# Where the second pieces of a Fourier step stand among the matmuls of a feed-forward layer (spectral mixer with a gated GELU branch, one core)

## The chip, the cores and the metric

The kernel runs on one core of a Trainium2 chip. The metric is the device time of one launch in microseconds (us); lower is better. Beside the plain runs there is one profiled execution, from which all traces are read.

## The reference

Inputs are `x` of 2 batches × 4096 tokens × 640 channels, the mixer weights `w1, b1, w2, b2` in four blocks of 160 channels, the feed-forward weights `w_gate, w_up` (640 × 1728) and `w_down` (1728 × 640), and a gate vector.

```python
g = sigmoid((x * gate_w).sum(-1, keepdims=True))
Xf = rfft2(x, axes=(1, 2))            # one row: a real transform over the 4096 tokens
# two complex block-diagonal layers on Xf: relu after the first, soft threshold 0.01 after the second
a = irfft2(Yf, s=(1, 4096), axes=(1, 2))
b = (gelu(x @ w_gate) * (x @ w_up)) @ w_down
return g * a + (1 - g) * b
```

## The kernel before

All matrix products run on TensorE with float32 operands that are split into a high and a low part, so each product of two matrices is three matmuls (high·high, high·low, low·high). A block product of one level of a Strassen-like scheme saves some of them. The high part is made by ScalarE (`high`, L274), the low part by VectorE (`low`, L277).

The kernel runs through these stages, and one program order per engine is written out by hand:

- **Up-projection.** `keys` (L1190) lists 48 passes, called keys here: three groups of weights (`groups`, L1189: 4, 4 and 6 column pairs), each with 16 token blocks. Keys 0 to 15 are the first group, 16 to 31 the second, 32 to 47 the third. A key runs `quad` (L487) once for each column pair (4, 4 and 5 times), and in the third group `mixed` (L559) once after its second quad. Key 0 runs `plain` instead. A quad issues 54 matmuls of 128x256, in seven products; a product is one call of `run` (L467) with 9 or 6 matmuls that add up in one PSUM bank. In the order of issue they are X (9), half5 of the quad before (9), C (9), A (6), X again (9), half3 of the quad before (6) and half4 of the quad before (6). All these matmuls have line L469 in the profile.
- **Stage A** is the first step of the Fourier transform. It has 64 token pairs (`a_seq`, L1192). Each needs an input load (`a_load`), two splits (`a_split`, one on each half of the partitions: a high of 64x640 on ScalarE and a low on VectorE), a gate sum (`a_gate`, VectorE), and two pieces (`a_step` with h=0 and h=1). A piece is two matmuls of 128x320 (L614), each followed by a ScalarE copy (L615) and a VectorE addition (L616); the second piece ends with a store. These are not a stage in time: they are put into the gaps between products of the up-projection.
- **Places.** A quad has seven hooks, one after each product or half; hook k of quad q of a key is slot 7q + k. `slots` holds what is called there. `A_POINTS` (L1235) gives the five slots of a token pair by weight group: split, split, gate, first piece, second piece. `steps_a` (L1246) says which key takes which token pair. The same slots carry the preparation of the next key's inputs (`x_prep`), of the next group's weights (`w_prep`) and of the down-projection's weights (`wd_pre`, in keys 33 to 46, at slots 12, 17, 22 and 27 of the odd keys and 1, 6, 11, ... 31 of the even ones).
- **PSUM.** There are eight banks. X and C of a quad and of the one before are open at the same time; A and each matmul of a piece take one more until VectorE has read them.
- **Queues.** SyncE issues most transfers; GpSimd issues the tables of stage A (`f1_load`, one for every 20 token pairs) and the stores of the prepared inputs in the first group.
- After key 47 follow the block-diagonal layers with the first inverse step, and then the second inverse step with the down-projection (`down`, L1139, which also uses `run`). The change moves nothing there.

Before, a key of the second group (17 to 30) has two token pairs and a key of the third group (33 to 44) has three; the first group has none. Both pieces stand at a hook, that is between two products.

Of the kernel before, what the change touches and what calls it, by code (L numbers as in the profile page):

```python
# [213 lines left out]
def spectral_mix_kernel(ctx: ExitStack, tc: tile.TileContext, a):  # L214
# [3 lines left out]
    def dr(t, off, ap):  # L218
        return bass.AP(tensor=t.tensor, offset=t.offset + off, ap=ap)
# [7 lines left out]
    def bank():  # L227
        return psum.tile([P, 512], F32, name="bank", tag="bank")
# [13 lines left out]
    def small(shape, dt=F32, name="small"):  # L242
        return pool.tile(shape, dt, name=name, tag="small", bufs=18)
# [7 lines left out]
    def st(dst, src):  # L251
        late.append((dst, src))
# [207 lines left out]
    def prod(ws, x):  # L460
# [3 lines left out]
            ops += [(wh, xh), (wh, xl), (wl, xh)]  # L464
        return ops

    def run(dst, ops, first=True):  # L467
        for i, (l, r) in enumerate(ops):
            nc.tensor.matmul(dst, l, r, start=first and i == 0, stop=i == len(ops) - 1, skip_group_check=True)  # L469

    def h_store(tp, t, h):
        st(dr(hD, 4 * tp * P * 14 * P + t * P, [[14 * P, P], [P * 14 * P, 4], [1, P]]),
           h.rearrange("p (t n) -> p t n", t=4))
# [13 lines left out]
    def quad(key, t, hook):  # L487
# [8 lines left out]

        X = half()
        run(X, prod(w["g1"], x_of(o, "b11", ("k4", 0))))
        p1 = T("p1")
        copy(p1, X)  # L500
        hook(0)
        old[0]()
        hook(1)
        C = half()
        run(C, prod(w["s3"], x_of(o, "t3", ("k4", 1))))
        hook(2)
        A = half()
        run(A, prod(w["g2"], x_of(o, "b21")))
        nc.vector.tensor_add(p1, A, p1)  # L509
        hook(3)  # L510
# [65 lines left out]
    def f1_load(q):  # L576
        m = min(5, 17 - 5 * q)
        F1[q] = big([P, 5, 2, P], F32R, name="f1")
        nc.gpsimd.dma_start(F1[q][:, :m], a["f1"][:, 5 * q:5 * q + m])
# [5 lines left out]
    def a_load(b, n2):  # L585
        t = small([P, D], name="xr")
        ld(t, a["x"][b, n2])
        XR[b, n2] = t

    def a_split(b, n2, h):  # L590

        t = XR[b, n2]
        xs = small([P, D], F32R, name="xs")
        hi, lo = (slice(0, 64), slice(64, P))[::1 - 2 * h]
        high(xs[hi], t[hi])
        low(xs[lo], t[hi], xs[hi])
        XS[b, n2, h] = xs

    def a_gate(b, n2):
        t = XR.pop((b, n2))  # L600
        nc.vector.scalar_tensor_tensor(t, t, 1.0, GW[0], op0=OP.mult, op1=OP.mult, accum_out=G[:, b, n2:n2 + 1])

    def a_step(b, n2, h):
        xs = XS.pop((b, n2, h))
        m = n2 if n2 < 16 else 32 - n2
        f = F1[m // 5][:, m % 5]
        if h == 0:
            XS[b, n2] = small([P, D], name="as")
        stg = XS[b, n2]
        hi, lo = (slice(0, 64), slice(64, P))[::1 - 2 * h]  # L610
        for q in range(2):
            cs = slice(320 * q, 320 * q + 320)
            pa = bank()
            nc.tensor.matmul(pa[:, :320], f[:, h], xs[:, cs], start=True, stop=True)  # L614
            nc.scalar.activation(stg[hi, cs], pa[lo, :320], AF.Copy)  # L615
            nc.vector.tensor_add(stg[hi, cs], pa[hi, :320], stg[hi, cs])  # L616
        if h:
            st(dr(scr1[b], n2 * D, [[32 * D, 4], [P * D, 32], [1, D]]), XS.pop((b, n2)))
# [613 lines left out]
    slots = {}  # L1232


    A_POINTS = {1: ((1, 3, 4, 5, 8), (12, 14, 16, 21, 23)), 2: ((0, 2, 3, 4, 9), (14, 15, 18, 18, 19), (24, 25, 27, 28, 29))}  # L1235

    points = lambda i: 7 * (5 if keys[i][0] == 2 else 4)

    def spread(i, s, fs):

        for k, f in enumerate(fs):
# [1 line left out]
            while j < last and q >= points(j):  # L1243
                j, q = j + 1, q - points(j)
            slots.setdefault((j, q), []).append(f)
    steps_a = [(i, j) for i in (*range(17, 31), *range(33, 46)) for j in range(2 if i < 33 else 3)][:64]  # L1246

    def back(i, s, f):
        if s < 0:
            i, s = i - 1, s + points(i - 1)  # L1250
        spread(i, s, [f])
    for k, (b, n2) in enumerate(a_seq):
        i, j = steps_a[k]
        sp = A_POINTS[keys[i][0]][j]
        if k in (0, 18, 38, 58):
            back(i, sp[0] - 12, lambda q=(k + 2) // 20: f1_load(q))
        back(i, sp[0] - 9, lambda b=b, n2=n2: a_load(b, n2))
        for s, f in zip(sp, (lambda b=b, n2=n2: a_split(b, n2, 0), lambda b=b, n2=n2: a_split(b, n2, 1),
                             lambda b=b, n2=n2: a_gate(b, n2), lambda b=b, n2=n2: a_step(b, n2, 0),
                             lambda b=b, n2=n2: a_step(b, n2, 1))):  # L1260
            back(i, s, f)
    for k in range(1, 4):
        spread(0, (0, 7, 14)[k - 1], w0[k][:2])
# [70 lines left out]
    for ch in range(1, 2 * NCH):  # L1334
        b, c = chunks[ch]
# [24 lines left out]
    for i in range(S + 2):  # L1360
# [18 lines left out]
        if 0 <= i - 1 < S:  # L1379
            b, c, n = steps[i - 1]  # L1380
# [66 lines left out]
```

## Time and profile before

| | us |
|---|---|
| median of 3 runs | 2575.9 (2572.92 to 2578.98) |
| profiled execution | 2586.86 |
| its span | 2585.1 |
| first and last piece of stage A (L614) start at | 446.0 and 1300.3 |
| TensorE busy in the span | 2568.1 |
| VectorE busy | 2062.9 |
| ScalarE busy | 1500.7 |
| GpSimd busy | 374.7 |

How to read it: the span is the time from the first to the last instruction of the profiled execution, and its own device time is 1.8 us longer. Matmuls are pipelined. A matmul is busy for some 280 ns, but the next one starts after less than half of that, so what counts for time is the distance from start to start, which a view gives as a stretch divided by the matmuls in it. A weight load (PEld) goes ahead of each matmul and overlaps the matmul before it. The granted clock is the share of its full clock that TensorE was given. A window of the trace also counts the instructions that were under way at its edges, so its counts are one or two above those that start in it.

### The profile page before, as it was taken

The numbers are of one execution on the slowest core, as the hardware profiler recorded it, in microseconds if no ns is written. First come the engines' busy times: TensorE is split into PE (matmuls) and PEld (weight loads), VectorE is DVE, ScalarE is ACT, GpSimd is POOL, SyncE is SP. The second block draws the span as 40 slices with busy tenths as digits, with TensorE's granted clock in tenths as the row PEclk, the third lists the DMA queues.
The fourth block names the chain that finished last, engine by engine and source line by source line (L and its number), as shares of the span: only waits on it lengthen the run. The fifth ranks groups of instructions, "written<-read, shape, count | busy, mean of one in ns | idle before, by whom it ended". The sixth has DMA issues, their size and how long they took to land.

```text
span 2585.1 us, 54281 instructions
## 1 busy us (share of the span) xinstructions
PE 2568.1 (99%) x20276; PEld 2560.5 (99%) x20276; DVE 2062.9 (80%) x4208; ACT 1500.7 (58%) x3490; POOL 374.7 (14%) x374
## 2 busy tenths in 40 slices
PE   9999999999999999999999999999999999999999
PEld 9999999999999999999999999999999999999999
DVE  7666567777778777777757788887899999999998
ACT  5444455666666566666645777777645444444443
POOL 0000000000000000000002111111233333333332
PEclk9999999999999999999999999999999999999999
DMA  6454547676667677776767354548744444344442
GB/s 216 161 192 164 188 166 236 205 239 212 218 213 250 197 231 232 242 222 218 237 202 222 121 165 142 162 141 249 284 148 154 153 145 141 130 153 153 146 135 99
DMA packets 341323, 483.48 MB, mean 187 GB/s; under 512 B 24572, under 2 KB 213500, under 8 KB 341060
## 3 DMA queue, kind: packets, MB, share of 16 engines
q1 hardware_dynamic: 326372, 438.47, 53.0%
q0 software_dynamic: 14688, 41.56, 4.4%
q8 instruction: 159, 2.61, 0.4%
q14 instruction: 104, 0.85, 0.1%
HBM read 300.29 MB, written 179.64 MB: 186 GB/s over the span
## 4 chain that ended last, share of the span: by engine, by line
PE 97%; DMA 1%; DVE 1%; ACT 0%; issue 0%; SPq 0%; DVEq 0%; ACTq 0%
PE bank L469 78%; PE bank L294 14%; PE bank L778 3%; PE bank L614 1%; PE bank L856 1%; PE bank L855 1%; DMA raw<-in_w1m_dram 0%; PE bank L858 0%; DMA zl<-zl 0%; DMA wx<-wdf 0%; DMA sc<-scr 0%; DMA rs<-in_w1s_dram 0%; DMA wraw<-in_wgu_dram 0%; DVE xo L278 0%; DVE s2s L278 0%
## 5 line engine op out<-in xcount | busy, mean ns | idle before, releaser
L469 PE MATMUL bank<-xo,w 128*128 128x256 f32 x11736 | 1390.9, 280 | 9.2 <-ACT xo L275 5.1
L469 PEld LDWEIGHTS bank<-xo,w 128*128 128x128 f32 x11736 | 1380.0, 189 | 12.3 <-ACT xo L275 5.1
L469 PE MATMUL bank<-wx,ho 128*128 128x320 f32 x4608 | 680.5, 309 | 0.0
L469 PEld LDWEIGHTS bank<-wx,ho 128*128 128x128 f32 x4608 | 676.7, 188 | 0.0
L493 ACT ACTIVATE u<-bank 128x256 f32<-128x256 f32 x408 | 156.0, 382 | 264.8 <-PE bank L469 259.1
L278 DVE TENSOR_TENSOR ho<-hraw,ho 128x640 fp32r<-128x640 f32 (+3 forms) x384 | 283.9, 780 | 5.1 <-ACT ho L275 3.1
L275 ACT ACTIVATE ho<-hraw 128x640 fp32r<-128x640 f32 x320 | 166.7, 574 | 63.3 <-PE bank L469 42.4
L493 ACT ACTIVATE p<-bank 128x256 f32<-128x256 f32 x204 | 78.3, 384 | 174.0 <-PE bank L469 80.7
L535 DVE TENSOR_TENSOR u<-bank,u 128x256 f32<-128x256 f32 x204 | 86.1, 422 | 98.7 <-PE bank L469 97.6
L526 DVE TENSOR_TENSOR u<-bank,u 128x256 f32<-128x256 f32 x204 | 86.1, 422 | 94.0 <-ACT u L493 91.2
L278 DVE TENSOR_TENSOR xo<-xraw,xo 128x512 fp32r<-128x512 f32 x209 | 143.0, 685 | 11.1 <-ACT xo L275 10.4
L1134 ACT ACTIVATE uu<-bank,gs 128x320 f32<-128x320 f32 x120 | 54.8, 524 | 161.5 <-PE bank L294 158.4
L278 DVE TENSOR_TENSOR xs<-xr,xs 64x640 fp32r<-64x640 f32 x128 | 105.0, 820 | 46.3 <-ACT xs L275 43.2
L616 DVE TENSOR_TENSOR as<-bank,as 64x320 f32<-64x320 f32 x256 | 113.9, 484 | 30.1 <-ACT as L615 28.8
L294 PE MATMUL bank<-wm,h 128*128 128x320 f32 (+1 forms) x792 | 137.8, 309 | 0.0
L275 ACT ACTIVATE xo<-xraw 128x512 fp32r<-128x512 f32 x209 | 130.8, 626 | 6.4 <-DMA xraw<-in_xT_dram 5.0
L567 POOL MEMSET h<- 64x512 f32 x16 | 8.3, 522 | 772.3 <-DMA xraw<-in_xT_dram 339.8
L294 PEld LDWEIGHTS bank<-wm,h 128*128 128x128 f32 (+1 forms) x792 | 118.6, 185 | 1.2
L509 DVE TENSOR_TENSOR p<-bank,p 128x256 f32<-128x256 f32 x204 | 86.1, 422 | 41.5 <-PE bank L469 38.7
L275 ACT ACTIVATE ho<-hs 128x640 fp32r<-128x640 f32 (+1 forms) x128 | 72.5, 579 | 79.7 <-PE bank L469 62.7
L278 DVE TENSOR_TENSOR s2s<-s,s2s 128x320 fp32r<-128x320 f32 x128 | 113.6, 944 | 0.4 <-ACT s2s L275 0.3
L615 ACT ACTIVATE as<-bank 64x320 f32<-64x320 f32 x256 | 96.7, 427 | 12.2 <-PE bank L614 9.6
(155 smaller groups left out, 3474.3 us busy)
## 6 DMA issues: line engine op xcount, KB each, us to landing
xo<-xD SPq DMA_DIRECT2D x124, 512.0 KB
xraw<-in_xT_dram SPq DMA_DIRECT2D x225, 256.0 KB
hD<-h SPq DMA_DIRECT2D x224, 256.0 KB
hraw<-hD SPq DMA_DIRECT2D x128, 320.0 KB
xD<-xo POOLq DMA_DIRECT2D x64, 512.0 KB, 3.2
sc<-scr SPq DMA_DIRECT2D x65, 320.0 KB
xr<-in_x_dram SPq DMA_DIRECT2D x64, 320.0 KB
scr<-as SPq DMA_DIRECT2D x64, 320.0 KB
```

Source lines behind the costliest of these rows:

```text
L275: nc.scalar.activation(dst, src, AF.Copy, scale=scale)
L278: eng.tensor_sub(dst, src, hi.bitcast(F32))
L294: nc.tensor.matmul(dst, l, r, start=i == 0, stop=i == len(ops) - 1)
L469: nc.tensor.matmul(dst, l, r, start=first and i == 0, stop=i == len(ops) - 1, skip_group_check=True)
L493: copy = lambda d, s_: nc.scalar.activation(d, s_, AF.Copy)
L509: nc.vector.tensor_add(p1, A, p1)
L526: nc.vector.tensor_add(u4, C, u4)
L535: nc.vector.tensor_add(u2, C, u2)
L615: nc.scalar.activation(stg[hi, cs], pa[lo, :320], AF.Copy)
L616: nc.vector.tensor_add(stg[hi, cs], pa[hi, :320], stg[hi, cs])
L778: nc.tensor.matmul(pz[:, kp * P:(kp + 1) * P], SC[b, c, kp][:, o:o + P], ft, start=True, stop=True)
L1134: nc.scalar.activation(uu[n2][:, cs], pe[:, :320], AF.Copy, scale=gs[:, b, 0, n2:n2 + 1])
```

## The change

Three edits. The second pieces are no longer called at their slot: they are put on the list `inner`, and the next call of `run` issues them right behind its first matmul, that is between the first two matmuls of a product. Ten token pairs go into keys 4 to 13 of the first group, one for each key, with the points of the first group of slots. Keys 33 to 45 of the third group then have two token pairs each instead of three in keys 33 to 44; the middle set of points (14, 15, 18, 18, 19) is dropped. The number of token pairs stays 64 and no matmul is added or removed.

```diff
+    inner = []
+
     def run(dst, ops, first=True):
         for i, (l, r) in enumerate(ops):
             nc.tensor.matmul(dst, l, r, start=first and i == 0, stop=i == len(ops) - 1, skip_group_check=True)
+            while inner and i == 0:
+                inner.pop()()
...
-    A_POINTS = {1: ((1, 3, 4, 5, 8), (12, 14, 16, 21, 23)), 2: ((0, 2, 3, 4, 9), (14, 15, 18, 18, 19), (24, 25, 27, 28, 29))}
+    A_POINTS = {0: ((1, 3, 4, 5, 8),), 1: ((1, 3, 4, 5, 8), (12, 14, 16, 21, 23)), 2: ((0, 2, 3, 4, 9), (24, 25, 27, 28, 29))}
...
-    steps_a = [(i, j) for i in (*range(17, 31), *range(33, 46)) for j in range(2 if i < 33 else 3)][:64]
+    steps_a = [(i, j) for i in (*range(4, 14), *range(17, 31), *range(33, 46)) for j in range(1 if i < 14 else 2)]
...
                              lambda b=b, n2=n2: a_gate(b, n2), lambda b=b, n2=n2: a_step(b, n2, 0),
-                             lambda b=b, n2=n2: a_step(b, n2, 1))):
+                             lambda b=b, n2=n2: inner.append(lambda: a_step(b, n2, 1)))):
             back(i, s, f)
```

## The prediction

> **What bounds the kernel.** I read the page first, then the groups of matmuls by stretch, then the order of time around the pieces of stage A, and last single weight loads.
>
> ```profile
> PE 2568.1 (99%) x20276; PEld 2560.5 (99%) x20276; DVE 2062.9 (80%) x4208; ACT 1500.7 (58%) x3490; POOL 374.7 (14%) x374
> PEclk9999999999999999999999999999999999999999
> PE 97%; DMA 1%; DVE 1%; ACT 0%; issue 0%; SPq 0%; DVEq 0%; ACTq 0%
> ```
>
> TensorE makes 97% of the chain of waits and hardly ever stops, at the full granted clock. The change adds and removes no matmul. So it can move the time only through the distance from one matmul to the next, or through new stops. The distance is not the same everywhere (first rows: windows, with the elapsed us, TensorE busy and its count in front; then the groups of 128x256 matmuls in the same three windows):
>
> ```profile
> 53.50:445.90 392.40, 392.40 (x3333) 392.35 (x3332) 251.13 (x570) 191.53 (x474) 29.76 (x56) 1.00 0.55 188
> 805.14:829.62 24.48, 24.48 (x218) 24.48 (x217) 20.09 (x55) 15.67 (x43) 0.00 (x0) 1.00 0.85 283
> 961.20:1382.60 421.40, 421.40 (x3548) 421.10 (x3547) 300.68 (x672) 253.35 (x602) 10.02 (x21) 1.00 0.71 228
> ...
> L469 PE MATMUL bank<-xo,w 128*128 128x256 f32 x3333 | 392.9, 281 | 0.0
> L469 PE MATMUL bank<-xo,w 128*128 128x256 f32 x218 | 24.9, 276 | 0.0
> L469 PE MATMUL bank<-xo,w 128*128 128x256 f32 x3429 | 414.1, 281 | 0.0
> ```
>
> The first window is 392.4/3332 = 117.8 ns a matmul. The second is key 31 with its 4 × 54 = 216 matmuls: 24.48/216 = 113.3 ns. The same shape has two paces, 4.5 ns apart, both at clock 1.00 (the number before the last two), and the busier DMA (0.85 against 0.55) goes with the fast one. The mean of one matmul, 281 or 276 ns, tells them apart. Slow are keys 1 to 16 and most of keys 35 to 46; the second group is fast throughout, from the first piece of stage A on.
>
> **What switches the pace.** This is matmuls in order of time at that first piece (start, length to the last end, count):
>
> ```profile
> 441.76 4.40 PE L469 MATMUL bank<-xo,w 128*128 128x256 f32 x36
> 446.00 0.45 PE L614 MATMUL bank<-xs,f 128*128 128x320 f32 x2
> 446.29 2.89 PE L469 MATMUL bank<-xo,w 128*128 128x256 f32 x24
> 449.02 0.45 PE L614 MATMUL bank<-xs,f 128*128 128x320 f32 x2
> ```
>
> Start to start it is (446.00 − 441.76)/36 = 117.8 ns before and (449.02 − 446.29)/24 = 113.8 ns after: two matmuls of a piece switched it. In the third group most pieces do not:
>
> ```profile
> 1001.60 0.45 PE L614 MATMUL bank<-xs,f 128*128 128x320 f32 x2
> 1001.89 1.23 PE L469 MATMUL bank<-xo,w 128*128 128x256 f32 x9
> 1002.95 0.45 PE L614 MATMUL bank<-xs,f 128*128 128x320 f32 x2
> 1003.24 9.35 PE L469 MATMUL bank<-xo,w 128*128 128x256 f32 x78
> 1012.43 0.45 PE L614 MATMUL bank<-xs,f 128*128 128x320 f32 x2
> ```
>
> After 1003.24 it is 9.19/78 = 117.8 ns still. What differs is the place in a beat of three. In the slow pace every third weight load takes 192 ns, the others 187 or 188. These are the first weight loads of the pieces at 446.00 and at 1001.60, each from a window that holds no other:
>
> ```profile
> L614 PEld LDWEIGHTS bank<-xs,f 128*128 128x128 f32 x1 | 0.2, 192 | 0.0
> ...
> L614 PEld LDWEIGHTS bank<-xs,f 128*128 128x128 f32 x1 | 0.2, 188 | 0.0
> ```
>
> I counted all pieces that started in the slow pace, 57 of them. Six have the 192 ns load first, and all six switch to fast. In 50 the 192 ns load stands just ahead of the piece; none switches, and the beat keeps its place in the products. One stands just ahead of the 192 ns load:
>
> ```profile
> 928.18 0.46 PE L614 MATMUL bank<-xs,f 128*128 128x320 f32 x2
> 928.48 1.22 PE L469 MATMUL bank<-xo,w 128*128 128x256 f32 x9
> 929.53 0.45 PE L614 MATMUL bank<-xs,f 128*128 128x320 f32 x2
> 929.82 2.44 PE L469 MATMUL bank<-xo,w 128*128 128x256 f32 x20
> ```
>
> After it the pace stays slow (929.53 − 928.48 is 1.05 us for 9, 117 ns), but the beat has moved forward by one matmul, and the next piece switches. All 71 pieces that started in the fast pace left it fast. All products have 6 or 9 matmuls, multiples of three, so between products the beat always meets a piece in the same place. The kernel before puts every piece there: a beat with the wrong place stays slow for good.
>
> **Edit 1, the second piece behind the first matmul of a product.** It adds no instruction. ScalarE's copy and VectorE's addition keep their place in their queues, since the product's own result comes later in any case. A piece there meets the beat one matmul further on. Call the place of the 192 ns load in a product 0, 1 or 2. By the three rules a first piece switches place 0, moves 1 to 0 and leaves 2; a second piece switches 1, leaves 0, and moves 2 to 1. So from any place, pieces in turn reach the fast pace in at most five. That the rules hold inside a product is taken from the stream of matmuls being the same there; no trace of before shows it.
>
> **Edit 2, ten token pairs in keys 4 to 13.** The first stands at about 115 us. Three weight loads in a row there, the first of them the first of a product:
>
> ```profile
> L469 PEld LDWEIGHTS bank<-xo,w 128*128 128x128 f32 x1 | 0.2, 187 | 0.0
> L469 PEld LDWEIGHTS bank<-xo,w 128*128 128x128 f32 x1 | 0.2, 192 | 0.0
> L469 PEld LDWEIGHTS bank<-xo,w 128*128 128x128 f32 x1 | 0.2, 187 | 0.0
> ```
>
> This is place 1. The first piece of key 4 moves it to 0, the second leaves it, the first of key 5 switches. Before, it was the same slot of key 17 that switched, 12 keys later: 12 × 216 × 4.5 ns = **−11.7 us** if the fast pace holds. A stop can end it. In the slow pace there is already one in key 14, where the next weights are prepared:
>
> ```profile
> 383.78 9.39 PE L469 MATMUL bank<-xo,w 128*128 128x256 f32 x77
> ```
>
> That is (9.39 − 0.28)/76 = 119.9 ns, 0.16 us of stops. No piece follows until key 17. If it turns the pace, some 62 us or 525 matmuls are slow again, +2.4 us; I take half, **+1.2**.
>
> What the ten pairs cost VectorE there (durations by group, then the same 8.5 us from the start of a key in the first and in the second group; VectorE is the third busy time):
>
> ```profile
> L616 DVE TENSOR_TENSOR as<-bank,as 64x320 f32<-64x320 f32 x256 | 113.9, 484 | 30.1 <-ACT as L615 28.8
> L278 DVE TENSOR_TENSOR xs<-xr,xs 64x640 fp32r<-64x640 f32 x128 | 105.0, 820 | 46.3 <-ACT xs L275 43.2
> L601 DVE SCALAR_TENSOR_TENSOR xr<-xr,gw 128x640 f32<-128x640 f32 x64 | 52.3, 818 | 0.5
> ...
> 185.80:194.30 8.50, 8.50 (x75) 8.50 (x74) 4.83 (x11) 3.65 (x9) 0.53 (x1) 1.00 0.58 213
> 646.80:655.30 8.50, 8.50 (x76) 8.50 (x76) 6.88 (x16) 5.47 (x12) 0.00 (x0) 1.00 0.69 247
> ```
>
> A token pair is 4 × 0.484 + 2 × 0.820 + 0.818 = 4.4 us, of which 3.4 fall into this stretch: 4.83 + 3.4 = 8.2 of 8.5 us. It is full, fuller than the 6.88 of the second group, so VectorE may run up to 1 us late. What waits for it first is half4, whose C bank VectorE must have read after half5; 30 matmuls lie between, 30 × 0.113 = 3.4 us. So I price this at nothing, with that cover; without it each key stops for what exceeds it. The pieces' own matmuls and transfers only move: 20 pieces leave the third group. The input loads (10 of 320 KB), stores and the first table on the GpSimd queue fall where DMA is busy 0.55 instead of 0.71.
>
> **Edit 3, two pairs a key in the third group.** The slow matmuls there are about the 3,370 of its 3,429 in the window above that are not in four short fast stretches, so 15 us at 4.5 ns is what can be had. How a fast stretch ends:
>
> ```profile
> 1034.81 4.20 PE L469 MATMUL bank<-xo,w 128*128 128x256 f32 x33
> 1038.84 0.45 PE L614 MATMUL bank<-xs,f 128*128 128x320 f32 x2
> 1039.13 1.19 PE L469 MATMUL bank<-xo,w 128*128 128x256 f32 x9
> 1040.16 0.45 PE L614 MATMUL bank<-xs,f 128*128 128x320 f32 x2
> ...
> L469 PE MATMUL bank<-xo,w 128*128 128x256 f32 x4 | 0.6, 276 | 0.0
> L469 PE MATMUL bank<-xo,w 128*128 128x256 f32 x68 | 8.2, 282 | 0.0
> ...
> 1040.91 0.87 DVE L616 TENSOR_TENSOR as<-bank,as 64x320 f32<-64x320 f32 x2
> ```
>
> The fast pace of 1041.1 is gone by 1041.7. In between, product A needed the bank that the addition at 1040.91 frees, about 0.06 us late. These are slots 28 and 29 of an odd key, which stay. The jam ahead of it does not: the dropped middle pair stood at 1029 us, and the 33 matmuls from 1034.81 took 4.03 us, 0.14 more than 33 × 117.8 ns. Over the odd keys I take **−1** for such stops. But in a whole fast key product A comes some 20 matmuls × 4.5 ns = 0.09 us earlier still, so I expect odd keys to fall back at slot 30. If the beat lands in place 2, as here, the next four pieces do not switch, and the first of the next odd key does: slow for 27 + 300 + 42 = 369 of 600 matmuls, which leaves 4 us of gain with the tail after key 45; in place 0 the next piece switches, 12 us. No stop at all gives 15. Between these I take **−6**, nearer to the row.
>
> **The sum.** −11.7 + 1.2 − 1 − 6 = −17.5 us. On the profiled execution, 2586.9 (2585.1 and 1.8 around the span), that is 2569; the median of the plain runs lies 11 us below that execution, so I forecast 2575.9 − 17 = **2559 us**.
>
> **Rivals.** *Fast everywhere*: the odd keys don't fall back and key 14 neither; −11.7 − 15 − 1 = −28, 2548. For it: with the middle pair gone VectorE is less loaded; against: the 0.06 us above is tied to a weight form at slot 27 that stays. *Stops keep breaking the first group*: the pieces there make and break the fast pace by turns, half of 11.7 is lost, and the third group gains little: −5, 2571. *The pace does not follow the beat*: one shape has one spacing in plain runs, or a piece inside a product does not act as between two; then nothing is gained, 2576. For it speaks only that the profiled execution is one of several; against it, six of six switches at the 192 ns load.
>
> The Trainium skill, TensorE: Matmul & The Clock Gate, section Back-to-back issue gap, gives a single spacing by the shape for an isolated matmul, N/2.4 + 2.5 ns, 109 ns for 256 columns; by that rule order is worth nothing and the time stays. The trace shows 113.3 and 117.8 ns for one shape, so it does not agree.
>
> *Slower*: VectorE in keys 4 to 13 is late by more than the 3.4 us of cover, since its 8.2 of 8.5 us come on top of what the quad before left over. Then half4 stops in the first or second quad of each of the ten keys, the fast pace is never kept in that group (0 instead of −11.7), and the third group gives −6. It decides from 0.6 us a key on; at 1.4 us it is +14 − 6 = +8, 2584. Against it: VectorE is idle in 43% of that stretch now.
>
> **Chances.** Forecast 0.40, fast everywhere 0.22, stops 0.15, no effect 0.11, slower 0.12. The range of 2545 to 2576 leaves out the slower case, half of no effect and a little below. A change within 0.2% (5.2 us) cannot be told from none here. Faster by more: 0.40 + 0.22 + 0.10 of the stops = 0.72; same 0.15 (the rest of the stops and most of no effect); slower 0.13.
>
> **What would show it.** Keys 6 to 13 at a mean of 276 ns a matmul from about 141 us on, and key 12 at about 25.1 us instead of 25.4; 276 ns in the second group as before; 281 ns in the third group only behind slot 29 of odd keys. It is wrong if keys 6 to 13 stay at 281 ns, if pieces inside products leave the fast pace, or if VectorE ends waits of L469 there.

## The result, and the profile after

| | before | after |
|---|---|---|
| median of 20 plain runs, us | 2575.4 (2562.2 to 2586.2) | 2563.0 (2558.8 to 2571.4) |
| ratio | | 0.9961 [0.9948, 0.9975] |
| profiled execution, us | 2586.9 | 2565.8 |
| its span, us | 2585.1 | 2564.0 |

The change makes the kernel faster: by 12.4 us in the medians, by 21 us between the two profiled executions. By the interval of the ratio, which is not the quotient of the two medians, the gain is 6 to 13 us. That the medians and the profiled executions differ is part of the explanation. The plain times of before are also spread twice as wide as those of after.

The page of after begins with these lines (first the busy times, then the granted clock by slices, then the chain by engine):

```profile
PE 2546.6 (99%) x20276; PEld 2539.7 (99%) x20276; DVE 2059.0 (80%) x4208; ACT 1502.7 (59%) x3490; POOL 376.4 (15%) x374
PEclk9999999999999999999999999999999999999999
PE 96%; DVE 2%; ACT 1%; DMA 1%; issue 0%; SPq 0%; POOL 0%; DVEq 0%; ACTq 0%; POOLq 0%
```

TensorE still sets the end, with the same 20,276 matmuls, at the same clock, but busy 21.5 us less. The groups of 128x256 matmuls of after in four stretches, 53 to 168, 172 to 790, 798 to 865 and 870 to 1359 us, show the pace (the mean of one matmul in ns stands behind the busy time):

```profile
L471 PE MATMUL bank<-xo,w 128*128 128x256 f32 x968 | 114.8, 281 | 0.0
L471 PE MATMUL bank<-xo,w 128*128 128x256 f32 x5257 | 609.0, 276 | 0.2 <-ACT u L497 0.2
L471 PE MATMUL bank<-xo,w 128*128 128x256 f32 x571 | 67.4, 281 | 0.0
L471 PE MATMUL bank<-xo,w 128*128 128x256 f32 x4173 | 482.8, 276 | 0.0
```

Slow up to 168 us, then fast, but for two keys behind 798 us. In before, 53 to 446 us and most of 961 to 1383 us were slow. The windows from key 5 to 16, and from key 33 to 46, first of before and then of after, give the size (in both kernels each window begins and ends 21 matmuls behind the first matmul of its key):

```profile
137.38:442.82 305.44, 305.44 (x2594) 305.39 (x2593) 196.00 (x449) 149.19 (x373) 22.32 (x42) 1.00 0.55 186
863.62:1377.96 514.34, 514.34 (x4347) 513.65 (x4345) 374.03 (x832) 311.46 (x734) 10.54 (x21) 1.00 0.71 226
```

```profile
139.17:440.26 301.09, 300.94 (x2631) 300.61 (x2630) 231.66 (x521) 176.42 (x427) 21.85 (x41) 1.00 0.62 205
863.52:1356.25 492.73, 492.73 (x4307) 492.73 (x4305) 333.45 (x752) 283.30 (x674) 9.51 (x19) 1.00 0.70 222
```

In the first pair of windows after has 36 matmuls of stage A more, 18 pieces, which take about 0.31 us each in the fast pace (two starts of 146 ns and some 20 ns in the matmuls behind them). Without them its 301.1 us are 295.5: 10.0 us gained although there is more to do. In the second pair it has 40 fewer, 20 pieces or 6.2 us; of the 21.6 us less, 15.4 are gained. Most of that is pace: in keys 33 to 46, 3,272 matmuls started 116 to 121 ns ahead of the next one in before (called slow matmuls below), and 163 in after. Shorter stops are 1.3 us of it: starts more than 128 ns apart cost 1.6 us there in before, over the 113 ns of the fast pace, and 0.2 in after.

### The profile page after: what moved, and what is told of

The parts are those of the page before. It is cut to its first block, busy times and chain, and to the rows that moved or that the text cites. A ratio compares the mean times of both kernels' runs of the same rounds, so it can differ in the third digit from the quotient of the medians.

```text
span 2564.0 us, 54276 instructions
## 1 busy us (share of the span) xinstructions
PE 2546.6 (99%) x20276; PEld 2539.7 (99%) x20276; DVE 2059.0 (80%) x4208; ACT 1502.7 (59%) x3490; POOL 376.4 (15%) x374
## 4 chain that ended last, share of the span: by engine, by line
PE 96%; DVE 2%; ACT 1%; DMA 1%; issue 0%; SPq 0%; POOL 0%; DVEq 0%; ACTq 0%; POOLq 0%
PE bank L471 77%; PE bank L294 13%; PE bank L782 3%; PE bank L618 1%; PE bank L860 1%; PE bank L859 1%; DMA rl<-in_w1l_dram 0%; PE bank L862 0%; DMA sc<-scr 0%; DVE w L278 0%; DVE ys L278 0%; ACT m L919 0%; DVE xo L278 0%; ACT ys L275 0%; DMA wraw<-in_wgu_dram 0%
## 5 line engine op out<-in xcount | busy, mean ns | idle before, releaser
L471 PE MATMUL bank<-xo,w 128*128 128x256 f32 x11736 | 1369.0, 278 | 7.9 <-ACT xo L275 5.2
L471 PEld LDWEIGHTS bank<-xo,w 128*128 128x128 f32 x11736 | 1359.6, 188 | 9.7 <-ACT xo L275 5.2
L456 POOL DMA_DIRECT2D xD<-xo x64 | 34.3, 536 | 486.0 <-DVE xo L278 398.9
```

The lines of the kernel that those rows point to most:

```text
L456: nc.gpsimd.dma_start(xD[key[1]][:, kept], XM.pop((key, name)).rearrange("p h n -> p (h n)").bitcast(F32))
```

## The experiments

Two theories stand against each other. *The beat*: in the slow pace every third weight load takes 192 ns, and a piece of stage A switches to the fast pace if its own first weight load is the one on the beat; the gain comes from where the pieces stand. *The load*: the gain comes from moving VectorE's and ScalarE's work from the third group of weights to the first, and so from fewer stops; one matmul more or less ahead of a piece is worth nothing.

### The kernel before, again

> The kernel before once more, for a second profile. Beat theory: the pace in keys 1 to 16 hangs on where the beat of three lands after a stop in the first keys, so another execution may differ: either slow to the first piece of key 17 (281 ns a matmul) as in the first profile, or slow even beyond it, or fast earlier; the third group is slow behind a stop until a stop moves the beat. The time then lies somewhere between 2562 and 2586 us, and its place in that range goes with the count of slow matmuls at 4.5 ns each. Load theory (stops by a busy VectorE make the time): the same picture as in the first profile, slow and fast stretches in the same keys, and the scatter of plain times has no counterpart in the pace.

The same program, 2587.6 us. Keys 1 to 13 were slow again. But the stops in key 14 left another beat, and the second group, fast in the first profile, was slow here up to a stop at 515 us. This is the order of matmuls where stage A begins, with 446.0 us in the first profile as its counterpart:

```profile
439.79 4.87 PE L469 MATMUL bank<-xo,w 128*128 128x256 f32 x40
444.50 0.45 PE L614 MATMUL bank<-xs,f 128*128 128x320 f32 x2
444.79 2.99 PE L469 MATMUL bank<-xo,w 128*128 128x256 f32 x24
447.62 0.45 PE L614 MATMUL bank<-xs,f 128*128 128x320 f32 x2
447.91 11.83 PE L469 MATMUL bank<-xo,w 128*128 128x256 f32 x99
459.57 0.45 PE L614 MATMUL bank<-xs,f 128*128 128x320 f32 x2
...
L614 PEld LDWEIGHTS bank<-xs,f 128*128 128x128 f32 x1 | 0.2, 187 | 0.0
```

Behind 447.91 it is 11.66/99 = 117.8 ns: the two pieces that follow the same products as in the first profile switch nothing. The last row is the first weight load of the piece at 444.50: 187 ns, where that of the piece at 446.00 took 192. The order of the program did not change; the beat did. The load theory has no room for this.

### The order alone, and the places alone

The first kernel has the list `inner` and `run` of after, with the token pairs where they were before:

```diff
-    A_POINTS = {0: ((1, 3, 4, 5, 8),), 1: ..., 2: ((0, 2, 3, 4, 9), (24, 25, 27, 28, 29))}
+    A_POINTS = {1: ..., 2: ((0, 2, 3, 4, 9), (14, 15, 18, 18, 19), (24, 25, 27, 28, 29))}
-    steps_a = [(i, j) for i in (*range(4, 14), *range(17, 31), *range(33, 46)) for j in range(1 if i < 14 else 2)]
+    steps_a = [(i, j) for i in (*range(17, 31), *range(33, 46)) for j in range(2 if i < 33 else 3)][:64]
```

> Second pieces behind the first matmul of a product, but all token pairs where they were before (two in keys 17 to 30, three in keys 33 to 44). Beat theory: keys 1 to 16 slow as before (281 ns), fast from key 17 or 18 at the latest, third group fast but for short stretches of at most five pieces, that is at most some 350 matmuls; gain of 8 to 14 us on the profiled span of 2585.1, about half to all of the median's 12 us, and the scatter smaller than that of before. Load theory: the order of one matmul is worth nothing; time as before, 2575 us, third group slow.

The second has the token pairs of after, with both pieces between products:

```diff
-                             lambda b=b, n2=n2: inner.append(lambda: a_step(b, n2, 1)))):
+                             lambda b=b, n2=n2: a_step(b, n2, 1))):
```

> Token pairs placed as in the changed kernel (ten in keys 4 to 13, two a key in the third group), but both pieces between products. Beat theory: a beat in place 1 or 0 is switched in keys 4 or 5 and then all is fast, 2558 to 2565 us; a beat in place 2 is never switched, and then up to 30 keys are slow at 0.97 us each, 2575 to 2595 us; plain times scatter over 20 us or more, median 2565 to 2580. Load theory: the load alone is what counts, so the whole gain is here: 2563 us with a small scatter.

| us | median | lowest, highest | ratio to before |
|---|---|---|---|
| before (26 runs) | 2584.5 | 2567.5, 2602.7 | |
| order alone (12 runs) | 2571.7 | 2561.0, 2578.7 | 0.9945 [0.9917, 0.9973] |
| places alone (12 runs) | 2563.1 | 2559.8, 2582.3 | 0.9935 [0.9907, 0.9963] |

Either part alone makes the kernel faster. The load theory has no room for the gain of the order alone, nor for two late runs of the places alone; but the median of the places alone, 2563.1, is the time that it named, and lies 2 us below the range that the beat theory gave. The twelve runs of the order alone fall into two clusters, five at 2561.0 to 2563.4 and seven at 2571.2 to 2578.7. That fits: there are no pieces in the first group, and what its first stop leaves stays. No run of the upper cluster was profiled. The profiled execution took 2562.0 us and belongs to the lower cluster; its matmuls from 55 to 380 us have 276 ns, where 281 were expected:

```profile
L471 PE MATMUL bank<-xo,w 128*128 128x256 f32 x2864 | 325.3, 276 | 0.1
```

The places alone have ten runs at 2559.8 to 2569.8 and two at 2579.9 and 2582.3. In the profiled execution the beat was in place 1 before key 4; the first piece moved it to 0 and the second, which stands between products here, switched:

```profile
114.43 0.46 PE L618 MATMUL bank<-xs,f 128*128 128x320 f32 x2
114.73 2.99 PE L471 MATMUL bank<-xo,w 128*128 128x256 f32 x24
117.55 0.45 PE L618 MATMUL bank<-xs,f 128*128 128x320 f32 x2
117.84 4.36 PE L471 MATMUL bank<-xo,w 128*128 128x256 f32 x37
...
L471 PE MATMUL bank<-xo,w 128*128 128x256 f32 x503 | 59.4, 281 | 0.0
L471 PE MATMUL bank<-xo,w 128*128 128x256 f32 x2243 | 257.9, 276 | 0.1
```

The last two rows are the groups of 55 to 114 us and of 120 to 380 us. That the two late runs are ones whose beat began in place 2 was expected, but neither of them was profiled.

The third group was fast in both, by different ways. Without the middle token pair no stop turned its pace; those of keys 34 to 44 were starts 143 to 146 ns apart. With three pairs a key one did, at 1016 us, and the pieces brought the fast pace back at 1035 us, with the third of them. In keys 33 to 46 the places alone left 118 slow matmuls and the order alone 347, while the four profiles of before have 1,900 to 3,272. So in the third group either part is enough, and shorter stops, which the load theory speaks of, are one of the two ways: they do not turn the pace. The change has both, and these runs do not tell which of them its gain there comes from.

### Behind the second matmul

```diff
-            while inner and i == 0:
+            while inner and i == 1:
```

> The changed kernel, but the second piece behind the second matmul of a product in place of the first. Beat theory: there a piece switches place 2, leaves 1 and moves 0 to 2. Place 2 then takes two pieces instead of five, place 1 four instead of three. From place 2 the fast pace comes in key 4 (about 120 us) instead of key 6 (168 us): 2 x 0.97 = 2 us less than the changed kernel, 2561 us; from place 1 half a key later, 2563.5 us. Scatter as small as that of the changed kernel. Load theory: the same time as the changed kernel to within 1 us, and no difference in where the pace switches.

Median 2562.7 us (2556.2 to 2566.3, 9 runs), ratio 0.9923 [0.9892, 0.9953] on the chip of the last table. After was not timed in those runs, so the 2 us could not be told. But the profile shows the whole cycle of the rule for this place. Behind the stops of key 30 the beat is in place 1; then come the pieces of key 33:

```profile
861.98 0.46 PE L618 MATMUL bank<-xs,f 128*128 128x320 f32 x2
862.28 4.99 PE L471 MATMUL bank<-xo,w 128*128 128x256 f32 x41
867.11 0.46 PE L618 MATMUL bank<-xs,f 128*128 128x320 f32 x2
867.40 20.42 PE L471 MATMUL bank<-xo,w 128*128 128x256 f32 x172
887.66 0.45 PE L618 MATMUL bank<-xs,f 128*128 128x320 f32 x2
887.95 1.46 PE L471 MATMUL bank<-xo,w 128*128 128x256 f32 x11
889.25 0.45 PE L618 MATMUL bank<-xs,f 128*128 128x320 f32 x2
889.54 2.66 PE L471 MATMUL bank<-xo,w 128*128 128x256 f32 x22
```

The first, between products, moves 1 to 0; the second, behind a second matmul, moves 0 to 2; the third leaves 2; the fourth switches, as written down: four pieces from place 1. (867.40 to 887.66 is 117.8 ns a matmul.)

### Both pieces inside

```diff
-                inner.pop()()
+                inner.pop(0)()
...
-                             ... lambda b=b, n2=n2: a_step(b, n2, 0),
+                             ... lambda b=b, n2=n2: inner.append(lambda: a_step(b, n2, 0)),
```

> The changed kernel with both pieces behind the first matmul of a product. Beat theory: now each piece switches place 1, leaves place 0 and moves place 2 to 1; so place 2 and 1 reach the fast pace within key 4, and place 0 is never switched by any piece. In a profile that starts in place 1 or 2: fast from key 4; in place 0: slow until some stop moves the beat. Plain times in two clusters, one at 2558 to 2566 us and one 10 to 25 us above. Load theory: one time, that of the changed kernel.

Median 2578.7 us (2569.1 to 2588.5, 12 runs), ratio 1.0025 [1.0003, 1.0047]: this order is slightly slower than before. In the profiled execution the beat was in place 1 first and the first piece of key 4 switched. The stops of key 30 left place 0, which pieces inside a product never switch, and all that came next left it there up to a stop at 891 us:

```profile
863.34 0.45 PE L618 MATMUL bank<-xs,f 128*128 128x320 f32 x2
863.62 4.76 PE L471 MATMUL bank<-xo,w 128*128 128x256 f32 x39
868.22 0.45 PE L618 MATMUL bank<-xs,f 128*128 128x320 f32 x2
868.51 20.66 PE L471 MATMUL bank<-xo,w 128*128 128x256 f32 x174
889.01 0.45 PE L618 MATMUL bank<-xs,f 128*128 128x320 f32 x2
889.30 1.23 PE L471 MATMUL bank<-xo,w 128*128 128x256 f32 x9
```

The same 64 token pairs, in the same keys as in after and with the first pieces one matmul away, are slower than before. So the load alone does not make the time. The case is not a clean one, though: the stops of the third group were longer here, up to 376 ns from start to start in the profile. In keys 33 to 46 they cost 3.9 us against 0.2 in after, and they turned the pace both ways. So not all of the loss is the pieces' missed switches. The two clusters that were expected are not clear: the times spread over 19 us.

### Matmuls without any load

To the kernel before, five pairs of matmuls are added in keys 2 and 3. They write to banks that nobody reads.

```diff
+    inner = []
+
+    def blank(i):
+        w, x = WG[0]["g1"][0][0], XO[keys[i]]["b11"][0]
+        for q in range(2):
+            nc.tensor.matmul(bank()[:, :320], w, x[:, :320], start=True, stop=True)
...
+            while inner and i == 0:
+                inner.pop()()
...
+    for i, s, within in ((2, 5, 0), (2, 8, 1), (2, 19, 0), (2, 22, 1), (3, 5, 0)):
+        f = lambda i=i: blank(i)
+        spread(i, s, [(lambda f=f: inner.append(f)) if within else f])
```

> The kernel before, with five pairs of 128x320 matmuls added in keys 2 and 3 whose results nobody reads (first, third and fifth between products, second and fourth behind the first matmul of a product). They add 5 x 0.31 = 1.6 us of matmuls and no work for VectorE, ScalarE or the queues; stage A stays where it was. Beat theory: from any place the five switch the pace, so keys 4 to 13 are fast (276 ns a matmul, 24.5 us a key in place of 25.44), 10 x 0.97 - 1.6 = about 8 us less than a run of the kernel before that is slow there; the third group slow as before. Load theory: 1.6 us longer than before, 281 ns in keys 4 to 13.

| us | median | lowest, highest | ratio to before |
|---|---|---|---|
| before (35 runs) | 2576.3 | 2560.9, 2585.1 | |
| blank pairs (12 runs) | 2567.2 | 2562.3, 2570.5 | 0.9975 [0.9957, 0.9993] |
| both inside (12 runs) | 2578.7 | 2569.1, 2588.5 | 1.0025 [1.0003, 1.0047] |
| early, behind second (12 runs) | 2561.7 | 2559.6, 2566.7 | 0.9952 [0.9934, 0.9970] |
| after again (12 runs) | 2564.2 | 2556.7, 2568.9 | 0.9970 [0.9950, 0.9990] |

Ten matmuls more, for no result, take 9 us off the median; by the interval of the ratio the gain is 2 to 11 us. They take nothing off the shortest times, the lowest being 1.4 us above that of before; they remove the long ones. 19 of the 35 runs of before took 2576 us or more, none of these twelve took over 2570.5. In the profiled execution the third group, which was expected to be slow, had only 840 slow matmuls in keys 33 to 46. For the switch it is a weak witness: it was fast before the first blank pair (54.77 to 62.81 us, 8.04/71 = 113.2 ns), so it cannot show that the pairs switch:

```profile
54.77 8.21 PE L476 MATMUL bank<-xo,w 128*128 128x256 f32 x71
62.81 0.45 PE L472 MATMUL bank<-xo,w 128*128 128x320 f32 x2
```

### Earlier pairs, and after again

```diff
-            while inner and i == 0:
+            while inner and i == 1:
...
-    steps_a = [(i, j) for i in (*range(4, 14), *range(17, 31), ...
+    steps_a = [(i, j) for i in (*range(2, 12), *range(17, 31), ...
```

> Second pieces behind the second matmul of a product, and the ten token pairs of the first group in keys 2 to 11 in place of 4 to 13. Beat theory: fast from key 2 or 3, that is two keys earlier, 2 us less than with keys 4 to 13: 2560 us; the range of plain times no wider than that of the changed kernel. Against it stands that VectorE still prepares weights in key 1 and 2: if the pieces stop there, more than 0.2 us a key, the 2 us are gone. Load theory: no gain, or a loss.

> The changed kernel once more, on the chip of these runs, for comparison with the other three and for a second profile. Beat theory: the switch in the first group comes in key 4, 5 or 6 after one, three or five pieces, by the place the first stop leaves; fast from there to key 30 but for short stretches behind stops; 2558 to 2566 us. Load theory: the same pace in the same keys as in the first profile.

The times are in the table above. The early variant has the lowest median of all, 2.5 us under that of after on the same chip, but the two intervals overlap, so it cannot be told from after. Both profiled executions were fast almost throughout, with some 450 slow matmuls each. After did not switch in keys 4 to 6 this time, because its first stop had not turned the pace at all; the expectation named only three of the four cases.

### Before, a third and a fourth time

> The kernel before a third time. Beat theory: its plain times fall into a cluster near 2564 us and one near 2580 us because the first stop leaves the pace fast or slow by chance. A profiled execution near 2565 us must show 276 ns a matmul in keys 5 to 13, one near 2585 us 281 ns; the count of slow matmuls differs by some 2,500 or more between the two. Load theory: 281 ns in these keys whatever the time.

> The same kernel as in the third run of before, a fourth execution: same expectation, fast or slow in keys 5 to 13 by chance, with the time that goes with it.

They took 2572.6 and 2567.4 us, and in both the first group was fast. The groups of 120 to 380 us in the four profiled executions of before, at 2586.9, 2587.6, 2572.6 and 2567.4 us:

```profile
L469 PE MATMUL bank<-xo,w 128*128 128x256 f32 x2209 | 260.3, 281 | 0.0
```

```profile
L469 PE MATMUL bank<-xo,w 128*128 128x256 f32 x2210 | 260.5, 281 | 0.0
```

```profile
L469 PE MATMUL bank<-xo,w 128*128 128x256 f32 x2289 | 260.3, 276 | 0.1
```

```profile
L469 PE MATMUL bank<-xo,w 128*128 128x256 f32 x2291 | 260.3, 276 | 0.2 <-ACT u L493 0.2
```

One program, two paces, and 80 matmuls more in the same 260 us. The second profile and the last two come from different chips, but one chip has shown both paces too: the order alone, whose instructions in keys 0 to 16 are those of before, was fast there on the chip of the second profile. Of the two clusters expected in the plain times, the 35 runs of before in the table above show a gap, with sixteen at 2560.9 to 2571.9 us and nineteen at 2576.1 to 2585.1; the twenty of the first table show none.

### All profiles together

Counted in each trace are the 128x256 matmuls of the up-projection whose start lies 116 to 121 ns ahead of the next one's:

| kernel | slow matmuls | span, us |
|---|---|---|
| after again | 446 | 2555.0 |
| early, behind second | 477 | 2558.5 |
| blank pairs | 1199 | 2561.1 |
| order alone | 1395 | 2560.2 |
| places alone | 1519 | 2559.2 |
| behind second | 1923 | 2562.3 |
| after | 2358 | 2564.0 |
| before, fourth | 2676 | 2565.6 |
| before, third | 3467 | 2570.8 |
| both inside | 3551 | 2570.5 |
| before | 6814 | 2585.1 |
| before, second | 7329 | 2585.9 |

A straight line through these twelve has 2554.3 us and 4.41 ns a slow matmul, and no span lies more than 2.1 us off it. The count alone gives the span of all these programs to within that, over a range of 31 us. I also counted every piece that met the slow pace in the twelve traces: of 42 whose first weight load was on the beat, 41 switched; of 195 right behind it, 191 left the beat in its place; of 16 right ahead of it, 15 moved it forward by one. Each of the six exceptions has a stop within the piece or right behind it, with starts 218 to 971 ns apart.

## Why the prediction was right, and where it was off

**The two paces and the switch.** Right, and the step that was taken on trust, that the rules hold inside a product, held: they describe pieces behind the first and behind the second matmul too. (Not all products have 6 or 9 matmuls: the two of `mixed` have 15. That is a multiple of three as well, so the argument stands.) The profile of after shows the longest way, from place 2 in five pieces. The first weight loads of the two pieces of key 4, the two of key 5 and the first of key 6:

```profile
L618 PEld LDWEIGHTS bank<-xs,f 128*128 128x128 f32 x1 | 0.2, 188 | 0.0
L618 PEld LDWEIGHTS bank<-xs,f 128*128 128x128 f32 x1 | 0.2, 188 | 0.0
L618 PEld LDWEIGHTS bank<-xs,f 128*128 128x128 f32 x1 | 0.2, 187 | 0.0
L618 PEld LDWEIGHTS bank<-xs,f 128*128 128x128 f32 x1 | 0.2, 188 | 0.0
L618 PEld LDWEIGHTS bank<-xs,f 128*128 128x128 f32 x1 | 0.2, 192 | 0.0
...
168.38 0.45 PE L618 MATMUL bank<-xs,f 128*128 128x320 f32 x2
168.67 3.00 PE L471 MATMUL bank<-xo,w 128*128 128x256 f32 x25
```

Only the fifth is on the beat. Behind 168.67 it is 2.84/25 = 113.6 ns.

**Edit 2.** Forecast −11.7 + 1.2 from key 5 to 16, measured −10.0. The fast pace came in key 6 and not in key 5, since the beat was in place 2 in this execution and not in place 1; the place is not a property of the program. From there on the sizes were right: key 12 took 25.11 us, where 25.1 was forecast. The stop of key 14 grew, to key 14's 25.14 us against the 24.48 of a fast key, but did not end the fast pace. The cover on VectorE held: its busy time in the window of these keys rose from 196.0 to 231.7 us, and no stop showed in keys 6 to 13.

**Edit 3.** The term that was mis-sized in the profile: −6 and −1, measured −15.4. The −1 for shorter stops was about right (1.3); the −6 for the pace was 14. I expected odd keys to fall back behind slot 29, from the stretch around 1041 us. They did not. In after the stop near that point was found in even keys, with starts 144 to 152 ns apart in place of 113, and the pace stayed fast; in before it was 170 ns. The price was right for a stop that turns the pace, but I had only one size of stop to go by.

**What no term had.** In key 30 the second piece stops within itself, and here that stop ended the fast pace:

```profile
795.93 0.31 PE L618 MATMUL bank<-xs,f 128*128 128x320 f32 x1
796.97 0.41 PE L618 MATMUL bank<-xs,f 128*128 128x320 f32 x1 [0.72 <-DVE as L620]
797.22 2.99 PE L471 MATMUL bank<-xo,w 128*128 128x256 f32 x24
```

Keys 31 and 32, without pieces, were slow, 571 matmuls or 2.5 us, until the first piece of key 33. And the slow pace began at 12 us, not 53, which cost 1.0 us; with two pieces more in key 4 it was 1.6 us in all by key 5.

**The sum.** −17.5 us was forecast against the profiled execution, where 21.1 were measured. In the plain runs it was 12.4. The step that failed is the last one: I took the 11 us between the profiled execution and the median for a constant. They were no constant. The profiled execution of before was one with a slow first group, and two of its four profiles have a fast one already; the spread of its plain times suggests that a good part of those have it too. A gain that is read from one execution holds for those alone whose beat fell the same way; in the others there is less to gain. That the plain runs of after ended between 2557 and 2571 us in two sets, where those of before reached 2585 and more, is what the change does. That 2559 came within 4 us of the measured 2563.0 is in part luck: the third group gave 8 us more than its terms, and the step to the plain runs took 9 us off again.

**The rivals.** *Fast everywhere* is what the third group did and what the second profile of after shows, at 2556.7 us; its −28 from the profiled execution of before is 2559, and its 2548 again took the 11 us for a constant. *Stops keep breaking the first group* did not happen in the profiles of after: the stops of key 14 left the pace fast. *The pace does not follow the beat*, and the single spacing by shape beside it, fell with the pieces counted above, 41 switches of 42 on the beat, and with the two paces of one shape in every profile. *Slower* did not come up: in keys 6 to 13 of after no two up-projection matmuls in a row start more than 126 ns apart.

## What to carry to other kernels

Where matmuls of one shape fill TensorE, look at the mean of one matmul by stretch before looking for idle time: here 281 instead of 276 ns is 4% of a stretch, at clock 1.00 and with TensorE busy throughout. An odd piece of work of another shape ended the slow pace here, but only from the right place modulo the period; two places that differ by one reached all three. And when plain times spread over 1%, take several profiles of the same program before pricing a change from one of them.

## What the runs showed of the hardware

The slow pace is a stable state of three matmuls, 353 ns in place of 340, with one weight load of 192 ns in each three. It begins at a stop, or, as at 12 us in after, where the first matmuls, 213 ns apart, give way to the closer spacing, and it can last for thousands of matmuls. Over the twelve traces, single starts up to 152 ns apart never turned the fast pace (43 stops), 170 ns always did (7 of 7), and 153 to 166 ns went both ways. Longer is not surer: of 38 single starts 173 to 218 ns apart ahead of key 47, eleven turned it. So length alone does not decide, and what else does was not found. The stop in the last quads of key 1 lies in the range that goes both ways. In ten of the profiles it was 152 to 164 ns long; it turned the pace in five of them, to all three places, and left it in five. That is where the spread of the plain times begins: a stop that costs 0.05 us by itself decides on some 10 us. What in TensorE keeps the state up was not found either. The Trainium skill, TensorE: Matmul & The Clock Gate, section Back-to-back issue gap, has the spacing of a stream of weight loads and matmuls set by both. A state that shows in the weight loads, 192 ns in place of 188, agrees with that; for the spacing itself the measured 113.3 and 117.8 ns decide.
